# Sliding-window attention into a two-layer block: V loaded in rows of eight tokens and moved to key spans on chip, q and k on 96 partitions, w_out in 8-KB runs

## The chip, the cores and the metric

The kernel runs on one core of a Trainium2 chip. The metric is the device time of one execution in microseconds, the median of several runs. Beside the runs one execution was profiled; the rows in this text come from it. Engines are written as in the profile: PE is the matrix engine and PEld its weight loads, DVE the vector engine, ACT the scalar engine, POOL the GpSimd engine, SP the queue that issues DMAs.

## The reference

Attention over 8 batches of 8 heads, 576 tokens and 64 channels, in which a token sees itself and the 63 tokens before it. Its output, 4608 tokens of 512 channels, goes through two matrices with `h - tanh(h)` between them.

```python
scores = (1 / sqrt(64)) * q @ k.transpose(0, 1, 3, 2)        # 8 x 8 x 576 x 576
mask   = (rel >= 0) & (rel < 64)                             # rel = query - key
attn   = softmax(where(mask, scores, -1e9))
x      = (attn @ v).transpose(0, 2, 1, 3).reshape(4608, 512)
h      = x @ w_in                                            # 512 x 2048
out    = (h - tanh(h)) @ w_out                               # 2048 x 512
```

All inputs and the output are float32; the kernel multiplies in bf16.

## The kernel before

The attention is done for 32 groups `g`, each two heads of one batch (`b, pr = divmod(g, 4)`). q and k of a group come by SP's DMAs (`load_qk`, line 72), 72 partitions of eight tokens, are cast to bf16 (line 82, on POOL but for the first), transposed by eight PE transposes each (`tr`, line 154) and copied out of PSUM to `qT` (lines 158 and 159, the one on ACT, the other on DVE) and `kT` (line 161, ACT). Queries are taken in nine blocks of 64, each against its own 64 keys and the 64 before them, so a block sees 128 keys: nine matmuls `sp` (line 168), three at a time, an Exp on ACT (line 170), one multiplication by the 0-or-1 mask on DVE (`masking`, line 174), and nine matmuls `ov` against V (line 181), three at a time, each followed by a reciprocal of the row sums and two multiplications on DVE (lines 184 and 187). V lies in `vw` with 128 keys on the partitions: the upper 64 partitions hold a block's own keys, loaded straight from HBM with a cast to bf16 by POOL's DMAs (`load_v`, line 91), one run of 64 channels for each key; the lower 64 hold the block before, copied from the upper ones by SP's DMA (`shift_v`, line 97). After each second group `x_tr` transposes the result into `xT` (lines 193 and 201).

The second half works on nine chunks `c` of 512 tokens. For each of 16 tiles `m` of the hidden layer `hp_mm` does four matmuls of 512 columns (`hp`, line 211), ACT takes the tanh (line 214) and DVE the difference `gT` (line 220). `yp_mm` does the second product, four matmuls a step and 16 matmuls to an output tile (line 228); `y_out` copies it on ACT (line 233) and stores it in two DMAs of SP (line 236). w_in and w_out come in four pieces each by POOL's DMAs with a cast (lines 103 and 107).

The order of all of this is written out by hand: time is counted in half steps `h`, two to a step `n = 16 c + m`. An even one does `hp` of step `n`, an odd one `yp` of step `n - 24` (LAG), and `at(h, ...)` adds the attention work in between. Batch 0's attention stands at negative `h`, ahead of the first `hp`; batch 1's is spread over 4 half steps a group, the later ones' over 8. Each engine runs its instructions strictly in the order in which they are written, and so do POOL's and SP's DMA issues. PSUM is shared out in pools: two buffers for `hp`, one for `yp`, two for transposes, two for `sp`, one for `ov`.

## Time and profile before

| | us |
|---|---|
| median of 3 runs | 398.25 |
| lowest and highest run | 393.59, 398.42 |
| the profiled execution's own time | 396.17 |
| its span, first to last instruction | 392.9 |
| PE busy in the span | 329.2 |
| DVE, ACT, POOL busy | 244.2, 184.8, 99.7 |

The profiled execution's time is 3.3 us more than its span; what lies around the span is the same program's start and end. The rows of the trace are in a section below. A row of a timeline begins with its start in us from the span's start and its length, then engine, line, operation, tiles, shapes and count, and in brackets how long the engine sat idle before it and what ended that. In a group of instructions the two numbers behind the bar are the busy time in us and the mean length of one in ns.

### The profile page before, as it was taken

To read this page: it belongs to the slowest core of one execution; us is meant where nothing else is said; L and a number is where in the kernel's file an instruction comes from. 1 tells how busy PE (TensorE), PEld (TensorE's weight loads), DVE (VectorE), ACT (ScalarE), POOL (GpSimd) and SP (SyncE) were. 2 spreads that over 40 slices of the span, in tenths; PEclk is the share of its full clock that TensorE was granted. 3 is DMA by queue.
4 is the path that set the end of the run, shared out by engine and by line. 5 is a ranking of instruction groups with operands and counts; after the bars stand their busy time and mean duration, and the time that the engine had idled before them with its cause. 6 is when DMAs were issued, how large, how long until landed. Compare 5 with 4: busy or idle time off the path is not lost.

```text
span 392.9 us, 6368 instructions
## 1 busy us (share of the span) xinstructions
PE 329.2 (84%) x2384; PEld 179.7 (46%) x2384; DVE 244.2 (62%) x553; ACT 184.8 (47%) x342; POOL 99.7 (25%) x107
## 2 busy tenths in 40 slices
...
GB/s 156 143 187 215 157 135 181 167 97 166 125 123 3 118 151 155 103 117 158 129 119 135 148 106 117 171 133 29 32 41 37 28 53 28 35 47 27 65 69 53
DMA packets 59006, 41.85 MB, mean 107 GB/s; under 512 B 39009, under 2 KB 43105, under 8 KB 58977
## 3 DMA queue, kind: packets, MB, share of 16 engines
q0 software_dynamic: 41536, 8.92, 61.0%
...
## 4 chain that ended last, share of the span: by engine, by line
PE 72%; DMA 13%; DVE 4%; issue 3%; POOL 3%; ACT 3%; SPq 0%; POOLq 0%; ACTq 0%
PE yp L228 32%; PE hp L211 29%; DMA vw<-vw 6%; DMA w_in_sb<-in_moe_w_in_dram 5%; PE ov L181 4%; PE sp L168 3%; PE tp L154 3%; DMA kf<-in_k_dram 2%; DVE xs L187 1%; PE tpx L193 1%; POOL kb L82 1%; DVE gT L220 1%; ACT ysb L233 1%; POOL vw L91 1%; ACT th L214 1%
## 5 line engine op out<-in xcount | busy, mean ns | idle before, releaser
L211 PE MATMUL hp<-xT,w_in_sb 128*128 128x512 bf16 x576 | 152.9, 389 | 3.0 <-DVE gT L220 2.2
L228 PE MATMUL yp<-w_out_sb,gT 128*128 128x512 bf16 x576 | 145.0, 379 | 4.3 <-ACT ysb L233 4.3
L214 ACT ACTIVATE th<-hp 128x512 f32<-128x512 f32 x144 | 86.0, 597 | 131.9 <-PE hp L211 111.4
L220 DVE TENSOR_TENSOR gT<-hp,th 128x512 bf16<-128x512 f32 x144 | 99.5, 692 | 58.8 <-ACT th L214 56.7
L211 PEld LDWEIGHTS <-w_in_sb 128*128 128x128 bf16 x576 | 53.2, 100 | 52.6 <-issue 8.9
L228 PEld LDWEIGHTS <-gT 128*128 128x128 bf16 x576 | 52.4, 98 | 54.0 <-issue 5.9
L181 PE MATMUL ov<-vw,pt 128*128 128x129 bf16 x288 | 36.5, 240 | 41.7 <-DMA vw<-vw 12.9
L187 DVE TENSOR_TENSOR xs<-ov,rc 64x192 bf16<-64x192 f32 x192 | 68.1, 355 | 4.6
L170 ACT ACTIVATE pt<-sp 128x384 bf16<-128x384 f32 x96 | 43.3, 489 | 32.1 <-PE sp L168 31.9
L181 PEld LDWEIGHTS <-pt 128*128 128x128 bf16 x288 | 23.9, 104 | 65.5 <-issue 26.2
L82 POOL CAST qb<-qf 72x1024 bf16<-72x1024 f32 x31 | 34.7, 1121 | 74.2 <-DMA qf<-in_q_dram 49.5
L91 POOL DMA_DIRECT2D vw<-in_v_dram x28 | 25.7, 924 | 68.4 <-PE ov L181 55.0
L82 POOL CAST kb<-kf 72x1024 bf16<-72x1024 f32 x31 | 34.0, 1096 | 20.9 <-DMA kf<-in_k_dram 20.1
L184 DVE RECIPROCAL rc<-ov 128x3 f32<-128x3 f32 x96 | 17.1, 178 | 34.0 <-PE ov L181 31.3
L233 ACT ACTIVATE ysb<-yp 128x512 f32<-128x512 f32 x36 | 21.5, 597 | 28.2 <-PE yp L228 28.2
L168 PE MATMUL sp<-qt,kt 128*128 128x128 bf16 x288 | 30.2, 239 | 1.3 <-ACT kt L161 1.1
L174 DVE TENSOR_TENSOR pt<-pt,mask 128x1152 bf16<-128x1152 bf16 x32 | 30.3, 946 | 0.9
L168 PEld LDWEIGHTS <-kt 128*128 128x128 bf16 x288 | 23.1, 108 | 10.1 <-ACT kt L161 1.8
L161 ACT ACTIVATE kt<-tp 128x576 bf16<-128x576 bf16 x32 | 20.7, 648 | 7.3 <-PE tp L154 7.3
L159 DVE COPY qt<-tp 64x576 bf16<-64x576 bf16 x32 | 14.7, 460 | 13.1 <-ACT qt L158 12.8
L158 ACT ACTIVATE qt<-tp 64x576 bf16<-64x576 bf16 x32 | 20.2, 634 | 0.8 <-PE tp L154 0.8
L154 PE MATMUL tp<-ident,qb 72*128 72x72 bf16 x256 | 14.9, 208 | 5.7 <-POOL mask L127 5.7
...
## 6 DMA issues: line engine op xcount, KB each, us to landing
...
```

The source lines that it names most:

```text
L82: eng.tensor_copy(o, i)
L91: nc.gpsimd.dma_start(out=vw[b % NV][64:128, p0:p1, :, 64 * i:64 * i + 64].rearrange("p r j d -> p (r j) d"), in_=v[b, NP * i + p0:NP * i ...
L154: nc.tensor.transpose(tp[:, e, :], src[:, e, :], ident[:P, :P])
L168: nc.tensor.matmul(sp[:, i, :], kT[g % NR][:, 64 * j:64 * j + 128], qT[g % NR][:, j].rearrange("c h t -> c (h t)"), start=True, stop=True)
L170: nc.scalar.activation(PT[g % NR][:, 3 * grp:3 * grp + 3, :], sp, ACT.Exp, scale=scale)
L174: nc.vector.tensor_tensor(p, p, mask.unsqueeze(1).to_broadcast([128, 2 * NJ, 64]), ALU.mult)
L181: nc.tensor.matmul(ov[:, i, :], PT[g % NR][:, j, :], vw[b % NV][:, pr, j, :], start=True, stop=True)
L187: nc.vector.tensor_tensor(xs[b % 2][r, 3 * grp:3 * grp + 3, pr, :], ov[r, :, r], rc[r].to_broadcast([64, 3, 64]), ALU.mult)
L211: nc.tensor.matmul(hp, w_in_sb[:, ki, m * 128:(m + 1) * 128], chunk_tile(c)[:, ki, :], start=(ki == 0), stop=(ki == 3))
L214: nc.scalar.activation(th, hp, ACT.Tanh)
L220: nc.vector.tensor_tensor(gT[c][:, m, :], hp, th, ALU.subtract)
L228: nc.tensor.matmul(yps[c, s], gT[c][:, m, s * 128:(s + 1) * 128], w_out_sb[:, m, :], start=(m == 0), stop=(m == M - 1))
```

## The change

q and k are taken six tokens to a partition, on 96 partitions, so that a transpose pair is six and six instead of eight and eight. V of two heads is loaded as float32 by POOL's DMAs, eight tokens to a partition on 72 partitions (`load_v`), cast into a bf16 tile `vb` that has a one behind each head's 64 channels (`cast_v`, on DVE for batch 0 and on POOL later), and brought to the key blocks by nine DMAs from SBUF to SBUF on SP (`keys_v`, 64 rows of 520 bf16 values each). The copy to the lower 64 partitions (`shift_v`) covers all eight heads in one DMA, for batch 0 in two DVE copies. w_out is loaded in runs of four whole rows, 8 KB; the hidden units are permuted to fit, so `hp`'s weights are every fourth column of w_in. w_in comes in three pieces. The nine `ov` matmuls of a group go to three PSUM banks and are followed by one reciprocal and two multiplications (`norm`). All of PSUM is one tile whose eight banks are named by number: 0 and 1 for `hp`, 2 for `yp`, 3 for transposes, 4 for scores, 5 to 7 for `ov`. An output tile is stored in one DMA. LAG goes from 24 to 16, and batch 0's attention with all early loads is written as one list of short codes (`play`), of which two lines are shown.

```diff
-    E, P = 8, S // 8
+    E, P = 6, S // 6
+    EV, PV = 8, S // 8
...
-    qk_pool = ctx.enter_context(tc.tile_pool(name="qk", bufs=4))
+    qk_pool = ctx.enter_context(tc.tile_pool(name="qk", bufs=3))
+    v_pool = ctx.enter_context(tc.tile_pool(name="v", bufs=4))
...
-    g_pool = ctx.enter_context(tc.tile_pool(name="g", bufs=3))
-    ps_hp = ctx.enter_context(tc.tile_pool(name="ps_hp", bufs=2, space=PSUM))
-    ps_yp = ctx.enter_context(tc.tile_pool(name="ps_yp", bufs=1, space=PSUM))
-    ps_tp = ctx.enter_context(tc.tile_pool(name="ps_tp", bufs=2, space=PSUM))
-    ps_s = ctx.enter_context(tc.tile_pool(name="ps_s", bufs=2, space=PSUM))
-    ps_ov = ctx.enter_context(tc.tile_pool(name="ps_ov", bufs=1, space=PSUM))
+    g_pool = ctx.enter_context(tc.tile_pool(name="g", bufs=2))
+    psum = ctx.enter_context(tc.tile_pool(name="psum", bufs=1, space=PSUM))
+    ps = psum.tile([128, 8, 512], F32, name="ps")
...
-    w_in_sb = const.tile([128, 4, d_ff], BF16, name="w_in_sb")
+    WIDE = 512, 512, 1024
+    w_in_sb = [const.tile([128, 4, n], BF16, name=f"wi{i}") for i, n in enumerate(WIDE)]
...
-    NV, NR = 2, 3
+    NR, NPT = 2, 4
...
+    vw = [const.tile([128, NJ, H, D + 1], BF16, name=f"vw{i}") for i in range(2)]
+    vb = const.tile([PV, EV, H, D + 1], BF16, name="vb")
+    PT = [const.tile([128, NJ, 128], BF16, name=f"pt{i}") for i in range(NPT)]
...
+    def move(eng, o, i):
+        if eng is nc.scalar:
+            nc.scalar.activation(o, i, ACT.Copy)
+        else:
+            eng.tensor_copy(o, i)
...
-    def load_v(b, p0=0, p1=NP):
-        for i in range(2):
-            nc.gpsimd.dma_start(
-                out=vw[b % NV][64:128, p0:p1, :, 64 * i:64 * i + 64].rearrange("p r j d -> p (r j) d"),
-                in_=v[b, NP * i + p0:NP * i + p1].rearrange("h (j p) d -> p (h j) d", p=64))
-    def shift_v(b, p0=0, p1=NP):
-        w = vw[b % NV].rearrange("p r j c -> p r (j c)")
-        nc.sync.dma_start(out=w[0:64, p0:p1, 129:], in_=w[64:128, p0:p1, :(NJ - 1) * 129])
-    w_in_r = moe_w_in.rearrange("(ko ki) f -> ki ko f", ki=128)
-    w_out_r = moe_w_out.rearrange("(ko ki) f -> ki ko f", ki=128)
-    def load_w_in(i):
-        nc.gpsimd.dma_start(out=w_in_sb[:, :, 512 * i:512 * i + 512],
-                            in_=w_in_r[:, :, 512 * i:512 * i + 512])
-    def load_w_out(i):
-        nc.gpsimd.dma_start(out=w_out_sb[:, 4 * i:4 * i + 4, :], in_=w_out_r[:, 4 * i:4 * i + 4, :])
+    def load_v(b, pr):
+        t = v_pool.tile([PV, 2, EV * D], BF16, tag="vf", name="vf")
+        nc.gpsimd.dma_start(out=t, in_=v[b, pr::NP].rearrange("h (p e) d -> p h (e d)", e=EV))
+        stage[b, pr, "v"] = t
+    def cast_v(b, pr, eng=nc.gpsimd):
+        move(eng, vb[:, :, 2 * pr:2 * pr + 2, 0:D].rearrange("p e h d -> p h e d"),
+             stage.pop((b, pr, "v")).rearrange("p h (e d) -> p h e d", d=D))
+    def keys_v(b):
+        for j in range(NJ):
+            nc.sync.dma_start(out=vw[b % 2][64:128, j].rearrange("p h c -> p (h c)"),
+                              in_=vb[8 * j:8 * j + 8].rearrange("p e h c -> p e (h c)"))
+    def shift_v(b, eng=None):
+        lo, hi = vw[b % 2][0:64, 1:NJ], vw[b % 2][64:128, 0:NJ - 1]
+        if eng is None:
+            nc.sync.dma_start(out=lo.rearrange("p j h c -> p (j h c)"), in_=hi.rearrange("p j h c -> p (j h c)"))
+        else:
+            eng.tensor_copy(lo[:, 0:4], hi[:, 0:4])
+            eng.tensor_copy(lo[:, 4:8], hi[:, 4:8])
+    w_in_r = moe_w_in.rearrange("(ko ki) f -> ki ko f", ki=128)
+    w_out_r = moe_w_out.rearrange("(i p r) d -> i p r d", p=128, r=4)
+    def load_w_in(i):
+        nc.gpsimd.dma_start(out=w_in_sb[i], in_=w_in_r[:, :, 512 * i:512 * i + WIDE[i]])
+    def w_in_tile(ki, m):
+        i = min(m // 4, 2)
+        f = 512 * (m // 4 - i) + m % 4
+        return w_in_sb[i][:, ki, f:f + 4 * 127 + 1:4]
+    def load_w_out(i):
+        nc.gpsimd.dma_start(out=w_out_sb[:, 4 * i:4 * i + 4, :], in_=w_out_r[i])
...
-    def tr(g, which):
+    def tr(g, which, bank, eng=nc.vector):
         src = rows.pop((g, which)).rearrange("p e h d -> p e (h d)")
-        tp = ps_tp.tile([128, E, P], BF16, tag="tp", name="tp")
+        tp = ps[:, bank, :].bitcast(BF16)[:, 0:E * P].rearrange("c (e p) -> c e p", e=E)
         for e in range(E):
             nc.tensor.transpose(tp[:, e, :], src[:, e, :], ident[:P, :P])
         if which == "q":
-            t = tp.rearrange("c e (j a) -> c j e a", a=8)
-            o = qT[g % NR].rearrange("c j h (e a) -> c j h e a", e=E)
-            nc.scalar.activation(o[0:64, :, 0], t[0:64], ACT.Copy)
-            nc.vector.tensor_copy(o[64:128, :, 1], t[64:128])
+            o = qT[g % NR].rearrange("c h (p e) -> c h p e", e=E)
+            t = tp.rearrange("c e p -> c p e")
+            nc.scalar.activation(o[0:64, 0], t[0:64], ACT.Copy)
+            move(eng, o[64:128, 1], t[64:128])
...
-    def scores(g, grp):
-        sp = ps_s.tile([128, 3, 128], F32, tag="s", name="sp")
+    def scores(g, grp, bank):
+        sp = ps[:, bank, 0:384].rearrange("p (i q) -> p i q", i=3)
         for i in range(3):
             j = 3 * grp + i
             nc.tensor.matmul(sp[:, i, :], kT[g % NR][:, 64 * j:64 * j + 128],
-                             qT[g % NR][:, j].rearrange("c h t -> c (h t)"), start=True, stop=True)
-        nc.scalar.activation(PT[g % NR][:, 3 * grp:3 * grp + 3, :], sp, ACT.Exp, scale=scale)
+                             qT[g % NR][:, :, 64 * j:64 * j + 64], start=True, stop=True)
+        nc.scalar.activation(PT[g % NPT][:, 3 * grp:3 * grp + 3, :], sp, ACT.Exp, scale=scale)
...
         b, pr = divmod(g, NP)
-        ov = ps_ov.tile([128, 3, 129], F32, tag="ov", name="ov")
         for i in range(3):
             j = 3 * grp + i
-            nc.tensor.matmul(ov[:, i, :], PT[g % NR][:, j, :], vw[b % NV][:, pr, j, :],
-                             start=True, stop=True)
-        rc = sm_pool.tile([128, 3, 1], F32, tag="rc", name="rc")
-        nc.vector.reciprocal(rc, ov[:, :, 128:129])
+            nc.tensor.matmul(ps[:, 5 + grp, 130 * i:130 * i + 130], PT[g % NPT][:, j, :],
+                             vw[b % 2][:, j, 2 * pr:2 * pr + 2, :], start=True, stop=True)
+    def norm(g):
+        b, pr = divmod(g, NP)
+        ov = ps[:, 5:8, 0:390].rearrange("p n (i h c) -> p n i h c", h=2, c=D + 1)
+        rc = sm_pool.tile([128, 3, 3, 1], F32, tag="rc", name="rc")
+        nc.vector.reciprocal(rc, ov[:, :, :, 0, D:D + 1])
+        xo = xs[b % 2].rearrange("p (n i) r d -> p n i r d", i=3)
         for h in range(2):
             r = slice(64 * h, 64 * h + 64)
-            nc.vector.tensor_tensor(xs[b % 2][r, 3 * grp:3 * grp + 3, pr, :], ov[r, :, r],
-                                    rc[r].to_broadcast([64, 3, 64]), ALU.mult)
-    def x_tr(b, half, w0, w1):
-        tp = ps_tp.tile([128, 5, 128], BF16, tag="tp", name="tpx")
+            nc.vector.tensor_tensor(xo[r, :, :, pr, :], ov[r, :, :, h, 0:D],
+                                    rc[r].to_broadcast([64, 3, 3, 64]), ALU.mult)
+    def x_tr(b, half, w0, w1, bank, eng=nc.vector):
+        tp = ps[:, bank, :].bitcast(BF16)[:, 0:640].rearrange("p (w t) -> p w t", t=128)
...
-            nc.vector.tensor_copy(o[:, half, :, lo - c * WPC:to - c * WPC],
-                                  tp[:, i0:i0 + to - lo].rearrange("p w (h t) -> p h w t", h=2))
+            move(eng, o[:, half, :, lo - c * WPC:to - c * WPC],
+                 tp[:, i0:i0 + to - lo].rearrange("p w (h t) -> p h w t", h=2))
...
-        hp = ps_hp.tile([128, TOK], F32, tag="hp", name="hp")
+        hp = ps[:, m % 2, :]
         for ki in range(4):
-            nc.tensor.matmul(hp, w_in_sb[:, ki, m * 128:(m + 1) * 128], chunk_tile(c)[:, ki, :],
+            nc.tensor.matmul(hp, w_in_tile(ki, m), chunk_tile(c)[:, ki, :],
...
         s, part = divmod(st, 4)
-        if part == 0:
-            yps[c, s] = ps_yp.tile([128, d_model], F32, tag="yp", name="yp")
+        yp = ps[:, 2, :]
         for i in range(4):
             m = 4 * part + i
-            nc.tensor.matmul(yps[c, s], gT[c][:, m, s * 128:(s + 1) * 128], w_out_sb[:, m, :],
+            nc.tensor.matmul(yp, gT[c][:, m, s * 128:(s + 1) * 128], w_out_sb[:, m, :],
                              start=(m == 0), stop=(m == M - 1))
     def y_out(c, s):
         ysb = sm_pool.tile([128, d_model], F32, tag="ysb", name="ysb")
-        nc.scalar.activation(ysb, yps[c, s], ACT.Copy)
-        for u in range(2):
-            r0 = c * TOK + s * 128 + 64 * u
-            nc.sync.dma_start(out=out[r0:r0 + 64, :].rearrange("(a e) d -> e a d", e=E),
-                              in_=ysb[64 * u:64 * u + 64, :])
+        nc.scalar.activation(ysb, ps[:, 2, :], ACT.Copy)
+        r0 = c * TOK + s * 128
+        nc.sync.dma_start(out=out[r0:r0 + 128, :], in_=ysb)
...
-    WIDE = dict(q=0, k=1, s0=4, s1=4, s2=6, mask=8, v0=10, v1=13, v2=15, x0=19, x1=22)
-    TIGHT = dict(q=0, k=1, s0=3, s1=3, s2=4, mask=5, v0=6, v1=7, v2=8, x0=10, x1=11)
...
+    at(-40, play, """
+        q0 v00 v01 v02 v03 i0 q1 c0ap d00d d01d d02d d03d q2 k0 T0 c1pp m0 S0 q3 M0 T1
+        s0d S1 w0 c2pp M1 V0 T2 q4 S2 V1 v10 v11 c3pp M2 T3 v12 v13 V2 S3 X0 M3 V3 X1
...
+        a = 4 * pr
+        at(a, tr, g, "q", 3, nc.scalar)
+        at(a + 1, tr, g, "k", 2)
+        for i in range(3):
+            at(a + 3 + i, scores, g, i, 4)
...
-    LAG = 16 + 8
+    LAG = 16
```

How the order changes at three places. First POOL's instructions from the start, in which `vw` and `vf` are V's tiles, `w_in_sb`, `wi` and `w_out_sb` the weights', and a CAST is one of q or k. Before:

```order
L91 DMA vw_94<-in_v_dram 64x9x64 x4
L125 MEMSET mask 128x64
L127 AFFINE_SELECT mask<-mask 128x64
L129 AFFINE_SELECT mask<-mask 128x64
L82 CAST qb<-qf 72x2x8x64
L82 CAST kb<-kf 72x2x8x64
L91 DMA vw_94<-in_v_dram 64x9x64 x2
L82 CAST qb<-qf 72x2x8x64
L82 CAST kb<-kf 72x2x8x64
L91 DMA vw_94<-in_v_dram 64x9x64 x2
L103 DMA w_in_sb<-in_moe_w_in_dram 128x4x512
```

And POOL's of the changed kernel, from the second piece of V's casts of batch 1 to the second piece of w_out:

```order
L78 COPY vb<-vf 72x2x8x64 x2
L126 DMA wi_85<-in_moe_w_in_dram 128x4x512
L78 CAST qb<-qf 96x2x6x64
L78 CAST kb<-kf 96x2x6x64
L126 DMA wi_86<-in_moe_w_in_dram 128x4x1024
L78 CAST qb<-qf 96x2x6x64
L78 CAST kb<-kf 96x2x6x64
L78 CAST qb<-qf 96x2x6x64
L78 CAST kb<-kf 96x2x6x64
L100 DMA vf<-in_v_dram 72x2x512 x2
L78 CAST qb<-qf 96x2x6x64
L78 CAST kb<-kf 96x2x6x64
```

V's casts now stand on POOL between the casts of q and k, and ahead of w_in's second and third piece.

Second DVE's from batch 0's first V casts (`vb`) on, in the changed kernel; `pt` is the Exp's result, `xs` the attention's output:

```order
L78 COPY vb<-vf 72x2x8x64 x4
L78 COPY qt_97<-ps 64x576
L147 MEMSET qt_98 128x576
L148 MEMSET kt_96 128x32
L150 MEMSET vw_88 64x520
L150 MEMSET vw_89 64x520
L190 TENSOR_TENSOR pt_91<-pt_91,mask 128x1152
L78 COPY qt_98<-ps 64x576
L118 COPY vw_88<-vw_88 64x2080
L119 COPY vw_88<-vw_88 64x2080
L190 TENSOR_TENSOR pt_92<-pt_92,mask 128x1152
L203 RECIPROCAL rc<-ps 128x9
```

Before, the first masking on DVE was followed by three rounds of a reciprocal and two multiplications, and V's casts and the copy to the lower partitions were in DMAs:

```order
L174 TENSOR_TENSOR pt_96<-pt_96,mask 128x1152
L184 RECIPROCAL rc<-ov 128x3
L187 TENSOR_TENSOR xs_105<-ov,rc 64x3x64 x2
L159 COPY qt_104<-tp 64x9x64
L184 RECIPROCAL rc<-ov 128x3
L187 TENSOR_TENSOR xs_105<-ov,rc 64x3x64 x2
```

DVE now does one round a group, and four casts and two copies of V for batch 0.

Third ACT's in batch 1's attention of the changed kernel, one group beside two steps of `hp` (`th` is the tanh; L174 and L76 are the two halves of `qT`, L177 is `kT`, L186 the Exp):

```order
L234 ACTIVATE th<-ps 128x512
L186 ACTIVATE pt_92<-ps 128x384
L234 ACTIVATE th<-ps 128x512
L186 ACTIVATE pt_92<-ps 128x384
L174 ACTIVATE qt_97<-ps 64x576
L76 ACTIVATE qt_97<-ps 64x576
L186 ACTIVATE pt_92<-ps 128x384
L177 ACTIVATE kt_95<-ps 128x576
```

Both halves of `qT` are ACT's there; before, one was DVE's (line 159).

## Rows read from the trace of the kernel before

**Rows 1.** Busy time of each engine in four stretches, granted clock, DMA.
```profile
core 0: us, PE busy (x) PEld busy (x) DVE busy (x) ACT busy (x) POOL busy (x), PEclk, DMA share, GB/s
0.00:51.00 51.00, 16.16 (x154) 12.66 (x155) 22.19 (x59) 12.68 (x22) 28.15 (x42) 1.00 1.73 168
51.00:118.50 67.50, 48.04 (x402) 27.69 (x401) 45.89 (x112) 32.62 (x65) 25.31 (x24) 0.85 1.76 142
118.50:362.50 244.00, 243.32 (x1740) 130.08 (x1737) 176.12 (x383) 135.93 (x250) 46.24 (x42) 1.00 0.71 89
362.50:392.90 30.40, 21.68 (x96) 9.26 (x95) 0.00 (x0) 3.58 (x6) 0.00 (x0) 0.97 0.19 60
```
**Rows 2.** The chain that ended last: start us, length us, what.
```profile
18.92 18.31 DMA w_in_sb<-in_moe_w_in_dram
...
50.30 16.33 DMA vw<-vw
...
86.61 8.60 DMA vw<-vw
...
118.62 0.87 PE yp L228 x4
```
**Rows 3.** POOL's DMA queue on the page: packets, MB, share of 16 engines' span.
```profile
q0 software_dynamic: 41536, 8.92, 61.0%
```
**Rows 4.** The same columns as rows 1, five microseconds of the loading.
```profile
25.00:30.00 5.00, 2.72 (x30) 2.46 (x29) 2.05 (x7) 2.57 (x5) 0.73 (x1) 1.00 1.18 259
```
**Rows 5.** Timeline: first landing, an issue of SP, a cast, V's arrival, the end.
```profile
2.54 0.40 SPq L72 DMA_DIRECT2D qf<-in_q_dram  x1
...
4.54 1.06 ACT L80 ACTIVATE qb<-qf 72x1024 bf16<-72x1024 f32 x1 [2.46 <-DMA qf<-in_q_dram]
...
6.16 0.69 DVE L82 CAST kb<-kf 72x1024 bf16<-72x1024 f32 x1 [1.50 <-DMA kf<-in_k_dram]
...
26.55 0.38 PE L181 MATMUL ov<-vw,pt 128*128 128x129 bf16 x2 [9.15 <-DMA vw<-vw]
...
51.10 3.16 PE L211 MATMUL hp<-xT,w_in_sb 128*128 128x512 bf16 x8
...
384.14 3.61 PE L228 MATMUL yp<-w_out_sb,gT 128*128 128x512 bf16 x16 [0.73 <-ACT ysb L233]
```
**Rows 6.** Groups of instructions: busy us, mean ns, idle before them and its releasers.
```profile
L220 DVE TENSOR_TENSOR gT<-hp,th 128x512 bf16<-128x512 f32 x144 | 99.5, 692 | 58.8 <-ACT th L214 56.7
L214 ACT ACTIVATE th<-hp 128x512 f32<-128x512 f32 x144 | 86.0, 597 | 131.9 <-PE hp L211 111.4 <-ACT pt L170 19.0 <-issue 1.5
L187 DVE TENSOR_TENSOR xs<-ov,rc 64x192 bf16<-64x192 f32 x192 | 68.1, 355 | 4.6
L211 PEld LDWEIGHTS <-w_in_sb 128*128 128x128 bf16 x576 | 53.2, 100 | 52.6 <-issue 8.9
L170 ACT ACTIVATE pt<-sp 128x384 bf16<-128x384 f32 x96 | 43.3, 489 | 32.1 <-PE sp L168 31.9
L82 POOL CAST qb<-qf 72x1024 bf16<-72x1024 f32 x31 | 34.7, 1121 | 74.2 <-DMA qf<-in_q_dram 49.5 <-issue 15.2 <-PE sp L168 4.2
L174 DVE TENSOR_TENSOR pt<-pt,mask 128x1152 bf16<-128x1152 bf16 x32 | 30.3, 946 | 0.9
L161 ACT ACTIVATE kt<-tp 128x576 bf16<-128x576 bf16 x32 | 20.7, 648 | 7.3 <-PE tp L154 7.3
L201 DVE COPY xT<-tpx 128x512 bf16<-128x512 bf16 (+4 forms) x46 | 15.4, 361 | 3.5 <-PE tpx L193 3.1
L159 DVE COPY qt<-tp 64x576 bf16<-64x576 bf16 x32 | 14.7, 460 | 13.1 <-ACT qt L158 12.8
```
**Rows 7.** Timeline: a cast on POOL beside a masking on DVE.
```profile
43.35 1.05 POOL L82 CAST qb<-qf 72x1024 bf16<-72x1024 f32 x1
43.38 2.61 DVE L174 TENSOR_TENSOR pt<-pt,mask 128x1152 bf16<-128x1152 bf16 x1
```
**Rows 8.** Timeline: weight loads of eight transposes.
```profile
58.19 0.33 PEld L154 LDWEIGHTS <-kb 72*128 72x128 bf16 x8
```

More of the change, by code (lines that the diff above doesn't have):

```diff
@@ L78, in cast @@
         i = stage.pop((g, n)).rearrange("p h (e d) -> p h e d", d=D)
-        if eng is nc.scalar:
-            nc.scalar.activation(o, i, ACT.Copy)
-        else:
-            eng.tensor_copy(o, i)
+        move(eng, o, i)
         rows[g, n] = t
@@ L139 @@
-    for pr in range(NP):
-        shift_v(0, pr, pr + 1)
+    def load_v(b, pr):
[9 more added lines that the diff above has]
+                              in_=vb[8 * j:8 * j + 8].rearrange("p e h c -> p e (h c)"))
```

149 lines of the change are left out of this document (91 added, 58 removed).

## The prediction, made before the change was run

> **What bounds the kernel now.** I read four stages first [rows 1]. From 118.5 to 362.5 us PE is busy for 243.3 of 244 us at the full granted clock; then 30 us in which it does the last second products alone. Nothing in the change makes a matmul shorter, so that part can only be had by starting it earlier. The first 118.5 us are the loose part: PE is busy for 16 of the first 51 us and for 48 of the next 67.5, at a mean clock of 0.85. What it waited for there is in the chain of waits [rows 2]: 18.3 us in a load of w_in, then 16.3 and 8.6 us in V's copy from the upper to the lower partitions. The timeline says the same of batch 0: its first matmuls against V go on at 26.55 us, after 9 us of waiting for that copy [rows 5]; the first `hp` is at 51.1 us, the first `yp` at 118.6 [rows 2, 5]. Behind it stands POOL's DMA queue: 41,536 packets for 8.9 MB, 61% of all 16 engines' span [rows 3], nearly all of them V's runs of 64 channels. So I cost the change as a shift of the first `yp`, and leave what follows nearly as it is.
>
> **V and the first loads, up to V in place.** The change asks first for six q and k loads and four of V, each 96 x 2 x 384 or 72 x 2 x 512 values of four bytes, 288 KB: 2.95 MB. The best five microseconds of the loading wrote 259 GB/s [rows 4], the first 51 us 168 [rows 1]: 11.4 or 17.6 us. Some of those 259 were weights, read at twice the bytes that they write, so the engines read more, and half of 11.4 is the lower end. I take 11.4, as V's packets are now 2 KB, and with the queue's start 12 us. V's last cast on DVE is 0.69 [rows 5], then SP issues nine DMAs at 0.4 each [rows 5], 3.6 us; the first load of all was in by 4.5 us [rows 5], so a small one's landing is under 3.7, and I take 2.5. The copy to the lower partitions is two DVE copies of 2080 columns; a masking of 1152 takes 0.95 [rows 6], so 1.7 each at its pace and 0.85 at twice that; half of it overlaps the last landings: 1 us. Sum 12 + 0.7 + 3.6 + 2.5 + 1 = 20 us, where before stands 26.55.
>
> **From there to the first `hp`.** Before, 24.5 us (26.55 to 51.1), a serial round of masking, three times `ov`, reciprocal and multiplications for each group. Now DVE has three maskings at 0.95, two copies of `qT` at 0.46, two of `xT` at 0.36 [rows 6], and four rounds of `norm`. A multiplication of 576 columns has no row: the one of 192 is 0.355, so at most 1.07; the difference `gT` of 512 columns is 0.69 [rows 6], so hardly less than that; 1.7 for two and the reciprocal. Sum 2.8 + 0.9 + 0.7 + 6.8 = 11.2 us. Beside it ACT needs 0.65 + 0.65 + 3 x 0.49 = 2.8 us a group [rows 6], hidden but for the first and the last: 4 us more.
>
> Here POOL comes in. It has V's loads and a dozen casts of 1.1 us in this stretch, and a cast on POOL beside a masking on DVE made the masking 2.61 us [rows 7], while the mean of all 32 is 0.95 [rows 6]. I add 1 us by that mean. The Trainium skill (SBUF — State Buffer, section "SBUF: two separate sides") has DVE and GpSimd share a pair of ports as an exclusive lock for a whole instruction. By that rule the loser always waits, by the mean it does now and then; the rule as a full price is rival two.
>
> First `hp`: 20 + 11.2 + 4 + 1 = 36 us. If DVE never waited it were 31; at the old 24.5 us it were 44.5. w_in's first piece is asked for early enough: by the order POOL issues it behind three casts and the mask, near 10 us, and at 259 GB/s its half megabyte takes 2 us.
>
> **Steps 0 to 7, beside batch 1's attention.** For each group, two steps, ACT has two tanh, three Exp, two halves of `qT` and `kT`: 2 x 0.60 + 3 x 0.49 + 2 x 0.65 + 0.65 = 4.6 us [rows 6]; PE has 2 x 0.87 [rows 2] and some 1.7 of attention, so it is hidden behind ACT. Four groups 18.4 us. The first `hp` will run slowly: before, eight matmuls took 3.16 us [rows 5], against 1.74 later; 1.4 more. Step 8 at 56 us. Without ACT's wait it were 14 us; at the old pace of this stage (24 steps in 67.5 us) 22.5.
>
> **Steps 8 to 15.** Now DVE is the longest: eight differences at 0.69, two maskings, two `norm` of batch 1, two `qT` copies and six of `xT`: 5.5 + 1.9 + 3.4 + 0.9 + 2.2 = 14 us. First `yp` at 70 us, if w_out is there. By then 7.1 MB of q and k, 3.5 of V, 4.2 of weights as written and 2.9 of keys and copies have to move: 17.7 MB in 70 us is 253 GB/s, just the 259 of rows 4, and w_out's last pieces stand on POOL behind V's casts of batch 2. I add 3 us: 73.
>
> **From the first `yp` to the end.** Before, 392.9 - 118.6 = 274.3 us. LAG 16 in place of 24 leaves eight more `hp` steps behind the first `yp`, 8 x 0.87 = 7 us. Attention: the 244 us held 120 steps of 2 x 0.87, 208.8 us, so 35.2 us for some 5.3 batches, 6.6 each; about a quarter batch more is left over now, 1.7 us. At the end PE stops 0.73 us between two output tiles [rows 5], four times and not six: -1.5. Sum 281.5. I put nothing on 96-partition transposes (six of 96 columns for eight of 72, the same columns) nor on the one store in place of two: PE is full, SP is not. `hp`'s weights are now read at every fourth column: PE loads 128 of them in 0.10 us [rows 6] behind a matmul of 0.22, so up to twice that costs nothing; rival four is the rest. In the full stretch DVE and ACT have slack (176 and 136 of 244 us [rows 1]), and POOL's new casts, four a batch at 1.1 us, have more (46 of 244).
>
> **The sum.** 73 + 281.5 = 354.5 us of span; the profiled execution's time is 3.3 over its span: 358 us, where that execution had 396.2. The median of the runs before is 398.25, 2 us higher than the profiled one; I let that be part of the range.
>
> **Rivals.**
> One: the loads stay the bound up to the first `yp`. For it: the 17.7 MB need a rate that only five microseconds of the old trace had, SP and POOL issue in order, and nine small DMAs with waits now stand ahead of q and k on SP. Against it: most of V's small packets are gone from the queue [rows 3]. At the old 168 GB/s it would be 105 us to the first `yp`, in the middle between 73 and that 88: 88 + 281.5 + 3.3 = 373 us.
> Two: DVE waits a whole cast of POOL each time. Three maskings, two copies and four casts of V before the first `hp`, nine times 1.1 us, 10 in place of my 1: 367 us. For it the 2.61 us [rows 7], against it the mean [rows 6].
> Three: one PSUM bank for all transposes. In the full stretch q's transposes are followed by k's in the same bank after one `yp` and one `hp`, 1.74 us. In that time ACT has a tanh and half of `qT`, then DVE the other half: 0.60 + 0.65 + 0.46 = 1.71 us. If each hand-over is 0.5 us late, k's alone cost 24 x 0.5 = 12 us (370), all three of a group 36 us: 394, no change.
> Four, the other side: weight loads at every fourth column take four times as long. 400 ns against 217 of a matmul, 183 x 576 = 105 us: 463 us. It decides from about 300 ns a load on, 84 ns over a matmul, 48 us in all, which is 2% above 398. For it: no row has such a load. Against it: eight loads of 128 columns took 0.33 us [rows 8], 41 ns each; four times that is 165 and stays hidden.
>
> **How the numbers follow.** My forecast 0.65; rival one 0.15, two 0.08, three 0.08 (half of it within 2%), four 0.04. The likeliest is 358. Downwards: loads at twice the rate (-6) and a first `hp` without waits (-5), the 3 us of loads gone: 344. Upwards: the old 24.5 us and the old pace of steps 0 to 7 (+8, +3) give 369, rival one 373 and a little over. Range 343 to 376; outside lie the slow end of rival one, half of three, and four. Faster by over 2%, about what a measurement of this kernel can tell from no change: 0.9; within 2%: 0.05, rival three in full and rival one at its worst; slower: 0.05, rival four and what I have not thought of.
>
> **What would show it.** In the changed trace: batch 0's first matmuls against V near 20 us, the first `hp` near 36, the first `yp` near 73, and from there some 281 us with PE busy throughout. POOL's queue should have under 10,000 packets in place of 41,536: V's runs were one for each of 8 x 8 x 576 keys, 36,864, and are now an eighth of that, 4,608 of 2 KB. Rival one shows as PE waiting for `vw` or `w_out_sb` between 36 and 90 us; two as maskings and V copies of 2 us; three as PE waiting for DVE or ACT at the transposes after 120 us; four as weight loads of `hp` over 217 ns and a PE step over 0.87 us. I am wrong at the root if the stretch behind the first `yp` is more than 5 us longer than 281, or if the first `yp` is past 90 us.

## The result, and the profile after

The changed kernel takes 379.76 us (median of 4 runs, 379.31 to 381.63) beside 395.92 us for the kernel before (390.52 to 398.42): a ratio of 0.9695, 95% interval 0.9611 to 0.978. (The ratio is not that of the two medians: executions of a kernel come in a faster and a slower state, and ratios compare the faster alone, here those of the kernel before at 390.52 and 393.59.) It is faster by 3%, where 358 us and 10% were forecast; 379.76 lies above the range of 343 to 376. The profiled execution took 379.83 us with a span of 378.1. (The section on the change calls V's staging tile float32. It is bf16: POOL's DMA casts on the way, and `cast_v` only moves.)

The same columns as [rows 1], cut where the first `hp` and the first `yp` stand now, then at 120 us:

```profile
0.00:43.40 43.40, 13.97 (x138) 12.16 (x139) 23.95 (x35) 12.53 (x24) 24.08 (x37) 0.88 0.84 171
43.40:82.70 39.30, 28.51 (x254) 17.52 (x253) 25.71 (x42) 26.75 (x52) 18.49 (x23) 0.95 0.90 196
82.70:120.00 37.30, 29.08 (x211) 16.55 (x208) 21.41 (x33) 16.66 (x32) 13.74 (x16) 0.91 0.63 140
120.00:348.00 228.00, 227.44 (x1558) 127.66 (x1556) 149.87 (x241) 126.11 (x233) 52.51 (x63) 1.00 0.43 106
```

The first `yp` came from 118.5 to 82.7 us, 36 us earlier, and the end by only 15. Behind 120 us PE is as full as before. The lost time lies in the third line: PE is busy for 29.1 of 37.3 us, and its clock is granted at 0.91. Before, nothing of this kind stood behind the first `yp`. The chain of waits, in order of time (start, length, what), answers to [rows 2]:

```profile
82.53 3.97 DMA vw<-vb
87.03 4.42 DMA vw<-vw
91.49 0.38 PE ps L196 x2
...
94.38 1.15 PE ps L231 x4
...
104.61 2.15 DVE pt L190
...
110.95 0.97 PE ps L247 x4
```

It is V again, of batch 2 now: the key transfers land at 86.5, SP issues the shift at 87.03, that lands after 4.4 us, and PE has waited 6.69 us. The masking of 2.15 us at 104.61 is another starved one, beside a copy and a cast of POOL; PE waited 1.52 us for it. `hp` at 94.38 takes 1.15 us for its four matmuls where 0.86 is usual: between 90 and 100 us the granted clock is 0.76, so part of that stretch ran at the lower of TensorE's two levels, 1.2 GHz, after PE had been idle. The row at 110.95 is the ninth `yp` step. From there 267.2 us are left, and before it were 274.4 us from the first `yp`, less eight closing steps of 0.87: 267.4. So the pace behind that point is the old one to 0.2 us, and all that the change gives is given ahead of it.

The timeline at the places of [rows 5] (start, length, engine, line):

```profile
14.19 6.54 SPq L110 DMA_DIRECT2D vw<-vb  x9
...
23.29 0.65 PE L196 MATMUL ps<-vw,pt 128*128 128x130 bf16 x4 [1.98 <-DVE vw L119]
...
43.41 0.63 PE L231 MATMUL ps<-xT,wi 128*128 128x512 bf16 x1
```

V of batch 0 is in place at 23.29 us (20 forecast); the first `hp` stands at 43.41 (36). Between them lies one masking, and POOL beside it, as in [rows 7]:

```profile
34.22 2.06 POOL L78 COPY vb<-vf 72x1024 bf16<-72x1024 bf16 x2 [1.86 <-DMA vf<-in_v_dram]
...
34.78 4.61 DVE L190 TENSOR_TENSOR pt<-pt,mask 128x1152 bf16<-128x1152 bf16 x1
36.23 0.78 POOL L126 DMA_DIRECT2D wi<-in_moe_w_in_dram  x1
...
37.00 0.84 POOL L78 CAST qb<-qf 96x768 bf16<-96x768 f32 x1
37.76 0.83 POOL L78 CAST kb<-kf 96x768 bf16<-96x768 f32 x1
38.53 0.76 POOL L126 DMA_DIRECT2D wi<-in_moe_w_in_dram  x1
...
39.44 0.83 PE L196 MATMUL ps<-vw,pt 128*128 128x130 bf16 x6 [5.59 <-DVE pt L190]
```

That masking has 0.75 us of work (what the shortest ones take). It ends at 39.39, 0.8 us behind the cast that ends at 38.59, and did not get in while POOL only issued a DMA from 36.23 on. Of the groups [rows 6] and the queue [rows 3]:

```profile
q0 software_dynamic: 8816, 8.92, 15.6%
...
L231 PEld LDWEIGHTS <-wi 128*128 128x128 bf16 x576 | 60.9, 114 | 46.7 <-issue 5.0
...
L207 DVE TENSOR_TENSOR xs<-ps,rc 64x576 bf16<-64x576 f32 x64 | 48.3, 755 | 1.5
```

The queue has a fifth of its packets, a strided weight load costs 14 ns more behind a matmul of 217, and the multiplications of a division take 48.3 us in all where they took 68.1.

### The profile page after: what moved, and what is told of

Read it like the earlier page. It is cut to its first block, busy times and chain, and to the rows that moved or that the text cites. A ratio compares the mean times of both kernels' runs of the same rounds, so it can differ in the third digit from the quotient of the medians.

```text
span 378.1 us, 6020 instructions
## 1 busy us (share of the span) xinstructions
PE 322.4 (85%) x2256; PEld 184.3 (49%) x2256; DVE 225.1 (60%) x355; ACT 188.7 (50%) x350; POOL 108.8 (29%) x139
## 4 chain that ended last, share of the span: by engine, by line
PE 71%; DVE 5%; DMA 2%; ACT 2%; issue 1%; ACTq 0%; SPq 0%
PE ps L247 32%; PE ps L231 28%; PE ps L196 3%; PE ps L170 3%; PE ps L184 3%; DVE gT L240 2%; DVE pt L190 2%; PE ps L213 1%; DMA vw<-vw 1%; ACT ysb L252 1%; DMA vw<-vb 1%; DVE xs L207 1%; ACT th L234 0%; DVE qt L78 0%; ACT qt L174 0%
## 5 line engine op out<-in xcount | busy, mean ns | idle before, releaser
L231 PE MATMUL ps<-xT,wi 128*128 128x512 bf16 x576 | 149.5, 382 | 3.3 <-DVE gT L240 3.0
L247 PE MATMUL ps<-w_out_sb,gT 128*128 128x512 bf16 x576 | 146.8, 381 | 3.0 <-ACT ysb L252 3.0
L240 DVE TENSOR_TENSOR gT<-ps,th 128x512 bf16<-128x512 f32 x144 | 99.2, 690 | 70.3 <-ACT th L234 69.0
L234 ACT ACTIVATE th<-ps 128x512 f32<-128x512 f32 x144 | 86.2, 598 | 83.9 <-PE ps L231 77.6
L231 PEld LDWEIGHTS <-wi 128*128 128x128 bf16 x576 | 60.9, 114 | 46.7 <-issue 5.0
L186 ACT ACTIVATE pt<-ps 128x384 bf16<-128x384 f32 x96 | 46.1, 490 | 56.0 <-PE ps L184 55.9
L78 POOL COPY vb<-vf 72x1024 bf16<-72x1024 bf16 x28 | 29.2, 1052 | 96.9 <-DMA vf<-in_v_dram 49.4
L207 DVE TENSOR_TENSOR xs<-ps,rc 64x576 bf16<-64x576 f32 x64 | 48.3, 755 | 1.5
L196 PE MATMUL ps<-vw,pt 128*128 128x130 bf16 x288 | 31.8, 230 | 19.3 <-DVE pt L190 9.6
L184 PE MATMUL ps<-qt,kt 128*128 128x128 bf16 x288 | 31.9, 228 | 15.3 <-DVE qt L78 11.4
L78 DVE COPY qt<-ps 64x576 bf16<-64x576 bf16 x28 | 21.3, 760 | 13.3 <-ACT qt L174 13.2
L174 ACT ACTIVATE qt<-ps 64x576 bf16<-64x576 bf16 x32 | 20.3, 635 | 9.0 <-PE ps L170 9.0
L177 ACT ACTIVATE kt<-ps 128x576 bf16<-128x576 bf16 x32 | 20.7, 646 | 7.5 <-PE ps L170 7.4
L78 DVE COPY xT<-ps 128x512 bf16<-128x512 bf16 (+4 forms) x42 | 14.5, 366 | 16.3 <-PE ps L213 16.0
```

Of the source, the lines that this page charges most:

```text
L78: eng.tensor_copy(o, i)
L184: nc.tensor.matmul(sp[:, i, :], kT[g % NR][:, 64 * j:64 * j + 128], qT[g % NR][:, :, 64 * j:64 * j + 64], start=True, stop=True)
L186: nc.scalar.activation(PT[g % NPT][:, 3 * grp:3 * grp + 3, :], sp, ACT.Exp, scale=scale)
L196: nc.tensor.matmul(ps[:, 5 + grp, 130 * i:130 * i + 130], PT[g % NPT][:, j, :], vw[b % 2][:, j, 2 * pr:2 * pr + 2, :], start=True, stop=True)
L207: nc.vector.tensor_tensor(xo[r, :, :, pr, :], ov[r, :, :, h, 0:D], rc[r].to_broadcast([64, 3, 3, 64]), ALU.mult)
L231: nc.tensor.matmul(hp, w_in_tile(ki, m), chunk_tile(c)[:, ki, :], start=(ki == 0), stop=(ki == 3))
```

## The experiments

Each kernel was timed beside the kernel before on one chip, but not all on the same chip. The median of the kernel before was 394.85 to 398.04 us there, so a difference of some 3 us between rows of different chips need not be the edit's.

| run | edit, to which kernel | us | ratio to before, 95% |
|---|---|---|---|
| e1_v2_first | V of batch 2 ahead of w_out, to the changed | 385.16 | 0.9726 (0.9658 to 0.9793) |
| e2_v1_on_act | two V copies to ACT, to the changed | 375.11 | 0.948 (0.942 to 0.954) |
| e3_both | e1 and e2 | 380.41 | 0.962 (0.9556 to 0.9683) |
| e9_pool_clear | e2 and two casts to ACT | 375.71 | 0.9476 (0.9414 to 0.9538) |
| r_after | the changed once more | 378.95 | 0.9644 (0.9572 to 0.9715) |
| e4_v_direct | V straight into place, to the changed | 372.36 | 365.29 to 375.03 us |
| r_v_direct | e4 once more | 370.28 | 0.9411 (0.9343 to 0.948) |
| e14_direct_c4_on_act | two casts to ACT, to e4 | 369.62 | 0.9423 (0.9351 to 0.9495) |
| e11_direct_pool_clear | four casts to ACT, V of batch 2 earlier, to e4 | 373.49 | 0.9381 (0.9304 to 0.9458) |
| e12_direct_v1_late | V of batch 1 behind w_in, to e4 | 374.07 | 0.9449 (0.9376 to 0.9522) |
| e13_v0_staged_only | batch 0's V staged, e9's order, to e4 | 375.19 | 0.9488 (0.9408 to 0.9568) |
| e7_before_lag16 | LAG 16, to the kernel before | 391.38 | 0.9892 (0.9826 to 0.9957) |
| e8_lag24 | LAG 24, to the changed | 388.39 | 0.9779 (0.9685 to 0.9873) |
| e6_w_out_2kb | w_out in 2-KB rows, to the changed | 378.81 | 0.956 (0.9497 to 0.9623) |
| e5_qk72 | q, k on 72 partitions, to the changed | 391.4 | 0.9906 (0.9865 to 0.9948) |
| e16_direct_qk72 | q, k on 72 partitions, to e4 | 378.24 | 0.9588 (0.9543 to 0.9634) |
| e18_direct_qk64 | q, k on 64 partitions, to e4 | 375.09 | 0.944 (0.9368 to 0.9513) |
| e17_one_bank_pv | one bank for `ov`, to e4 | 400.74 | 1.0111 (1.0059 to 1.0162) |

**Is the wait for batch 2's V a matter of order?** First theory: V of batch 2 is late because w_out's pieces and other work stand ahead of it.

```diff
-    ... w2 c6pp s1 q8 c7pp q9 v20 v21 c8pp o0 c9pp o1 v22 v23 d20p d21p o2 qa d22p d23p o3 qb k2 s2
+    ... w2 c6pp v20 v21 v22 v23 s1 q8 c7pp q9 d20p d21p d22p d23p k2 c8pp o0 c9pp o1 qa s2 o2 o3 qb
```

> The changed kernel with batch 2's V loads, V copies and key DMAs put ahead of w_out's loads in the list. Theory Order (V of batch 2 comes late because it stands behind w_out and the q and k casts on POOL): the 6.7 us in which PE waits for vw near 85 us are gone, PE stays at the full clock there, step 24 comes 8 to 9 us earlier (near 102 us), total near 371 us. Theory Rate (the DMA engines are full up to the first yp): PE waits for w_out_sb instead, total 378 to 380 us.

Both theories fell: 385.16 us, slower than the changed kernel, and PE did not wait for w_out instead. The rows of the matmuls against V in its trace, with what ended PE's idle time (us, times):

```profile
DMA vw<-vw: 9.7, 2
DVE pt L190: 8.2, 4
```

There are two waits for the copy now, 4.45 us at 61.5 (batch 1, whose transfers run beside the new loads) and 5.23 at 127.6 (batch 3); the one near 90 us is gone. Moving the loads moved the wait. The same with the edit below (e3_both) read 380.41 us and waited 4.62 us for V at 121.2.

**What the starved masking costs.** Two copies of V of batch 1 go from POOL to ACT; then (e9) two casts of q, k too, and both w_in issues ahead of the casts:

```diff
-    ... S2 V1 v10 v11 c3pp M2 T3 v12 v13 V2 S3 X0 M3 V3 X1 d10p d11p c4pp d12p d13p q5 q6 k1 w1 c5pp q7 w2 c6pp s1 ...
+    ... S2 V1 v10 v11 c3pp M2 T3 v12 v13 V2 S3 X0 d12a d13a M3 V3 X1 d10p d11p c4pp q5 q6 k1 w1 c5pp q7 w2 c6pp s1 ...   e2
+    ... S2 V1 v10 v11 c3pp M2 T3 c4aa v12 v13 V2 S3 X0 d12a d13a M3 V3 X1 d10p d11p q5 q6 k1 w1 w2 c5pp c6pp q7 s1 ...   e9
```

> The changed kernel with the second half of batch 1's V copies on ACT, ahead of the last masking of batch 0, in place of POOL. Theory Port (a masking on DVE waits for POOL's casts): the 4.6 us masking becomes less than 1.5 us and the first hp comes at 39 to 40 us in place of 43.4. By Port alone the total falls to 376 us; by Order the total stays at 379 to 380 us, since V of batch 2 lands as late as before and PE only waits longer for it. If the masking stays at 4 us or more, POOL is not its cause.

> On top of the kernel that casts two pieces of batch 1's V on ScalarE, the casts of q,k group 4 go to ScalarE too, both w_in issues stand ahead of the casts of groups 5 and 6, so that GpSimd has no back-to-back run of casts beside the masking of group 2. Theory (a masking does not start while GpSimd's casts follow each other without a gap): the masking of group 2 takes 0.75 to 1.2 us and not 4.4; first hp 41 to 42.5 instead of 45.3; the whole time 371 to 374 us. Rival (the masking was long for another reason, such as waiting for its data or for the transfers beside it): the masking keeps more than 2.5 us wherever the casts stand, first hp 44 or later, time 375 to 377.

Neither ending of e2 came whole. It took 375.11 us, 4 to 5 less than the changed kernel, but its first `hp` stood at 45.3, later than the 43.41 there. What it gained lies behind the first `yp`: the wait for batch 2's V is 1.96 us in place of 6.69, and the eight steps from there took 20.5 us in place of 28.2. In e2 the masking of group 3 was short, but that of group 2 took its place (start, length, DVE and POOL):

```profile
31.72 4.42 DVE L190 TENSOR_TENSOR pt<-pt,mask 128x1152 bf16<-128x1152 bf16 x1
...
33.72 0.83 POOL L78 CAST qb<-qf 96x768 bf16<-96x768 f32 x1
34.48 0.83 POOL L78 CAST kb<-kf 96x768 bf16<-96x768 f32 x1
35.25 0.76 POOL L126 DMA_DIRECT2D wi<-in_moe_w_in_dram  x1
```

With POOL kept clear, in e9:

```profile
31.04 1.53 POOL L126 DMA_DIRECT2D wi<-in_moe_w_in_dram  x2
...
31.20 1.17 DVE L190 TENSOR_TENSOR pt<-pt,mask 128x1152 bf16<-128x1152 bf16 x1
...
87.15 0.38 PE L196 MATMUL ps<-vw,pt 128*128 128x130 bf16 x2 [4.30 <-DMA vw<-vw]
```

So a masking took 1.17 us beside two DMA issues of POOL, and 4.42 beside its casts in a row, and the first `hp` stood at 41.5 against 45.3, as forecast. It is not a rule without exceptions: in the changed kernel the masking at 30.50 us took 1.18 beside two copies and two casts in a row, and in the kernel before one at 161.88 us took 1.60 beside two DMA issues alone. But the time stayed: 375.71 beside e2's 375.11, and not the 371 to 374 of the theory. The last row shows why: e9 waits 4.30 us for batch 2's V, where e2 waited 1.96. The unedited kernel says something else. 

> The changed kernel once more, unedited, beside the next two. Theory and rival alike: 379 to 381 us, a wait of PE for batch 2's V of 4.5 to 7 us near 90 us.

```profile
PE ps L196 <- DMA vw<-vw: 7.0, 2, 4.7
```

The median is 378.95 us, no other than the first. In its profiled execution the maskings of groups 2 and 3, beside the same copies as before, took 1.09 and 1.04 us, so the order alone does not decide whether one starves. The first `hp` stood at 40.70 and not 43.41, and PE waited for V 4.68 us at 58 (batch 1) and 2.33 at 90 us. That execution took 376.14 us, the shortest of the six and 3.7 less than the first profiled one. So a gain ahead of the appointment with V (the place in the written order where PE asks for it) was lost at it in e9 and kept here; the wait for V is there in both, 7.0 and 6.69 us in all.

**V without its staging.** V is cast by the DMA straight to its keys, in the small packets of before; the nine transfers and the copies go:

```diff
-        t = v_pool.tile([PV, 2, EV * D], BF16, tag="vf", name="vf")
-        nc.gpsimd.dma_start(out=t, in_=v[b, pr::NP].rearrange("h (p e) d -> p h (e d)", e=EV))
+        for i in range(2):
+            nc.gpsimd.dma_start(out=vw[b % 2][64:128, :, 2 * pr + i, 0:D],
+                                in_=v[b, NP * i + pr].rearrange("(j p) d -> p j d", p=64))
...
-            at(32 * b - 78 + 6 * pr, load_v, b, pr)
+            at(32 * b - 72 + 3 * pr, load_v, b, pr)
```

The last two lines also move the loads of batches 3 and on, so the runs with V straight into place price the staging together with the places of its loads.

> The changed kernel with V cast straight from HBM into its place by key, in packets of 128 B as before the change, without the staged rows, the nine key transfers and the vb copies. Theory (the V part carries what LAG does not): first hp at 47 to 51, waits of PE for vw in the first 120 us, time 387 to 392. Rival (the nine transfers, the copies and the starved maskings give back all that the longer packets gain): time 376 to 382.

> The kernel with V straight into place once more, unedited, with more rounds. Theory (the staged V is late for batch 2, and V in small packets is not): no wait for vw near 90 us or one under 4 us, the median 5 us or more under that of the changed kernel beside it. Rival (the first look was low by chance): the two medians within 3 us.

My theory of e4 had the wrong sign, and its rival's 376 was still too long. V straight into place is 8.7 us faster than the change that was to speed it up (370.28 beside 378.95 on one chip, intervals apart). Columns as above, for r_v_direct and then for the changed kernel, over the same stretches:

```profile
0.00:45.00 45.00, 14.57 (x138) 12.99 (x140) 18.68 (x32) 13.26 (x26) 26.40 (x41) 0.98 1.85 172
45.00:84.00 39.00, 29.08 (x257) 18.17 (x261) 24.76 (x42) 27.69 (x53) 22.01 (x30) 0.97 1.79 177
84.00:120.00 36.00, 34.16 (x263) 20.12 (x266) 25.85 (x45) 20.16 (x38) 14.37 (x18) 1.00 1.01 140
```

```profile
0.00:45.00 45.00, 15.31 (x141) 12.59 (x142) 24.09 (x35) 13.30 (x26) 24.08 (x37) 0.87 0.84 172
45.00:84.00 39.00, 28.46 (x258) 17.81 (x257) 25.79 (x42) 27.12 (x52) 18.49 (x23) 0.97 0.89 194
84.00:120.00 36.00, 27.78 (x200) 15.82 (x199) 21.19 (x33) 15.53 (x30) 13.74 (x16) 0.91 0.62 139
```

The small packets keep the DMA engines twice as busy (1.85 against 0.84) at the same 172 GB/s. Only the start waits for it:

```profile
PE ps L193 <- DVE vw L114: 11.7, 1, 11.7
```

V of batch 0 is in place at 27.3 us instead of 23.29, and the first `hp` stands at 45.0 instead of 43.41. Up to 84 us the two are alike again; then PE is busy for 34.2 of 36 us against 27.8, at the full clock. The first `yp` stands at 82.2 and 82.7, the wait for batch 2's V is 1.45 us against 6.69, and from the first `yp` to the end it is 286.5 us against 295.4.

On this kernel the first `hp` was tried once more, by `c4aa` behind T3 in place of `c4pp`: 

> The kernel with V straight into place, with the two casts of q,k group 4 on ScalarE in place of GpSimd, and nothing else moved. Theory (a first hp that comes earlier is kept where V of batch 2 is not late): the masking of group 2 takes under 1.7 us, first hp 43 to 45 instead of 46.2, time 1 to 3 us under the kernel with V straight into place. Rival (the appointment that counts is a later one): the same time within 1 us, whatever the first hp.

The masking took 1.25 us and the first `hp` came at 43.4, as expected; the time is 0.7 us less, which does not part theory from rival. Three other orders, e11_direct_pool_clear, e12_direct_v1_late and e13_v0_staged_only, read 373.5 to 375.2: none gained. Of these only e12 tells something by itself. It puts V of batch 1 behind w_in as before the change: 

> The kernel with V straight into place, but batch 1's V issued behind w_in's second and third piece, as in the kernel before the change. Theory (it is the place of batch 1's V among the loads, and not the form of its packets, that took away the wait for it of before): PE waits 5 us or more for vw between the first hp and the first yp, which are 44 us or more apart instead of 37.5; time 380 to 388 us. Rival (the loads have room behind the first hp either way): no wait over 2 us, time 370 to 376.

The rival held: no wait between the first `hp` and the first `yp`, which are 37.6 us apart. V's place among the loads is not what took the old wait away; what did, no run here shows. (e12 waits 3.4 us for batch 2's V at 89 us.)

**What carries the gain, then.** LAG, `LAG = 16` in the kernel before and `LAG = 16 + 8` with a third `g` buffer in the changed one:

> The kernel before with LAG 16 in place of 24, nothing else. If the earlier yp is a gain of its own, because steps 16 to 24 leave PE time for eight yp steps of 0.87 us each: 389 us. If those steps have no room, or w_out is late for them: 396 us, no change. If yp in between delays the attention of batch 2: above 396 us.

> The changed kernel with the distance between hp and yp put back from 16 to 24 steps (and the third g buffer that this needs). Theory (from the first yp on each pair of steps costs the same, so steps taken before it without a yp beside them are lost): 4 to 7 us slower, 384 to 387. Rival (a longer lead covers the wait for batch 2's V, 6.7 us, and so pays for itself): 376 to 381.

391.38 us and 388.39: LAG is worth 5.2 us on the one kernel and 8.6 on the other (6.9 without the longest of e8's four runs, 392.24; 7 forecast); the longer lead did not pay for itself. w_out by `"(i r p) d -> i p r d"`, with weights of 128 adjacent columns:

> The changed kernel with w_out read in rows of 2 KB and w_in's columns in order (no permuted rows, weights of 128 adjacent columns). Theory (the runs of w_out and the order of the columns lie beside other work): weight loads of hp go back from 114 to 100 ns, the time stays at 378 to 381 us and the first yp within 1 us of 82.7. Rival (the 8-KB runs bring the first yp forward, or relieve the queue that batch 2's V stands in): first yp or the wait for batch 2's V later by 3 us or more, time 383 to 387.

378.81 us; weight loads of 99 ns; the first `yp` at 84.3, as its first `hp` stood at 45.5. The runs and the permutation are worth nothing here, in either direction. Then the rows of q and k, `E, P = 8, S // 8` in place of 6, with V staged and with V direct, and 9:

> The changed kernel with q and k on 72 partitions (eight tokens a row, eight transposes a tile) instead of 96 (six). Theory (the 96 partitions save two transposes a tile and some of each copy, beside other work behind the first hp and 1 to 2 us ahead of it): 380 to 384 us. Rival (they carry much of the change's gain, through ACT and DVE in the stretch with batch 1's attention): 386 to 392 us.

> V straight into place and q,k on 72 partitions, so that of the change there remain the order of the first loads, the one set of banks, the distance of 16 steps and w_out's runs. Theory (the 96 partitions bring q, k and what stands behind them in earlier, whatever the form of V): 376 to 384 us, first hp or first yp 3 us or more later than the 45.0 and 82.2 of V straight into place with 96 partitions. Rival (they gain 12 us only because the staged V is late and every delay of it is paid): 369 to 373 us.

> V straight into place and q,k on 64 partitions, nine tokens a row. Theory (a load uses as many of the 16 DMA engines as divide its rows: 16 for 96 rows and for 64, 12 for 72): between 5 and 10 us the DMA engines write 220 GB/s or more, as with 96 rows (233) and not as with 72 (170), and the first cast of q on ScalarE starts at 4.1 to 4.3 us and not at 4.5; the whole time is open, since GpSimd's casts are longer on fewer partitions. Rival (the more rows the faster): 170 GB/s or less there, the first cast at 4.5 us or later, time above the 378 us of 72 rows.

With 72 partitions the changed kernel takes 391.4 us, and with V direct 378.24 instead of 370.28: 12 and 8 us, where the prediction put nothing. The rival held in e5, where PE waits 16.3 us for V in place of 6.7, and the theory in e16, with the first `hp` at 47.9 and the first `yp` at 87.1. Between 5 and 10 us of the program, on 96, 72 and 64 partitions (V direct; r_v_direct, e16, e18), the last column is GB/s:

```profile
5.00:10.00 5.00, 1.30 (x12) 0.97 (x12) 0.59 (x1) 1.13 (x3) 4.52 (x8) 1.00 1.30 233
```

```profile
5.00:10.00 5.00, 1.30 (x16) 1.05 (x16) 0.60 (x1) 1.47 (x3) 4.89 (x8) 1.00 1.74 170
```

```profile
5.00:10.00 5.00, 1.29 (x18) 1.07 (x18) 0.60 (x1) 1.77 (x3) 4.93 (x8) 1.00 1.41 212
```

72 rows load at 0.73 of the rate of 96, and 64 at 0.91. That more rows are always faster is thereby ruled out, and 64 rows gave the shorter time too (375.09). The theory came short on its other number: 212 and not 220, and the first cast of q at 4.80 us, later than the 4.51 of 72 rows. The Trainium skill (DMA: Bandwidth & Descriptors, section "Why a DMA increments its semaphore by 16 and not by 1") has a transfer use the largest number of engines up to 16 that divides its rows: 12 for 72, 16 for 96 and 64. The 0.73 agrees with 12/16; the 0.91 and the late first cast it does not explain, and they stay open. Fewer rows also make POOL's casts longer: 1.04 us on 72, 0.83 on 96, 1.16 on 64. How much of the 8 to 12 us is the load rate and how much these casts, no run parts: on 64 rows the first `hp` stood at 41.8 us, ahead of the 45.0 on 96, and yet the time is 4.8 us longer than there.

Last the three banks for `ov`: all three products of a group into bank 5, each divided before the next.

```diff
-            nc.tensor.matmul(ps[:, 5 + grp, 130 * i:130 * i + 130], ...
+            nc.tensor.matmul(ps[:, 5, 130 * i:130 * i + 130], ...
+        nc.vector.reciprocal(rc, ov[:, :, 0, D:D + 1])
+            nc.vector.tensor_tensor(xs[b % 2][r, 3 * grp:3 * grp + 3, pr, :], ov[r, :, h, 0:D], rc[r].to_broadcast([64, 3, 64]), ALU.mult)
```

> V straight into place on 96 partitions, but the three products of a group against V go into one PSUM bank, each divided before the next is written, as in the kernel before (two multiplications of 64 x 192 and a reciprocal three times a group, not two of 64 x 576 and one). Theory (the three banks took away PE's waits for DVE's multiplications, some 1.1 us twice a group, in front of the first yp): PE waits for xs of 1.0 to 1.2 us twice a group again up to the first yp, the first yp 6 us or more later than 82.2, time 376 to 384 us. Rival (ACT or the loads set the pace there anyway): first yp within 3 us, time 369 to 374.

400.74 us: 30 us, far over the theory's 6 to 14. Its timeline has the wait twice a group, and the waits of PE over 120 to 350 us (us in total, times, longest) show what the theory left out:

```profile
67.15 0.33 PE L193 MATMUL ps<-vw,pt 128*128 128x130 bf16 x3 [1.03 <-DVE xs L200]
68.51 0.42 PE L193 MATMUL ps<-vw,pt 128*128 128x130 bf16 x3 [1.03 <-DVE xs L200]
```

```profile
PE ps L193 <- DVE xs L200: 8.7, 32, 0.5
```

The first `hp` is at 53.1 and the first `yp` at 99.8, 8.1 and 17.6 us later; behind it PE now waits in the full stretch as well. DVE also has more to do in e17, 240.3 us in all in place of 213.3, and no run parts that from the bank itself. The kernel before had one bank too, with its products at other places: it lost nothing in its full stretch [rows 1], and waited some 1.1 us for the multiplications ahead of its first `yp`. So 30 us is the price of one bank, with its shorter multiplications, within the new order, and not what three would have given to the kernel before.

## Why the prediction was wrong

Its sum was 73 + 281.5 + 3.3. Measured: 82.7 + 295.4 + 1.7.

- **V in place, 20; it was 23.3.** The step that failed is "nine DMAs at 0.4 each", 3.6 us: SP took 6.54 us, 0.61 to 1.05 each. The 0.4 was the row of a load of 72 rows, and these move 64 pieces of 1040 bytes. The loads were in at 13.2 us where 12 was put, and the last copy of V took 0.97 where 0.69 was put; the landing and the last copy to the lower partitions gave 1 us back.
- **First `hp`, 36; it was 43.4.** Of the 7.4 us, 3.3 come from the step above and 4.1 from the way on. There the three maskings took 6.55 us, one of them 4.61, where 3.85 was put, the 1 us for POOL included. That is rival two, put at its mean. That POOL's work beside it makes a masking long is borne out by e2 and e9, but the price is another than one cast each time: a row of them or, as at 30.50 us, hardly any. The row behind the price had it already. The cast of [rows 7] ends at 44.40, and the masking goes on to 45.99, past a second cast:

```profile
44.33 1.05 POOL L82 CAST kb<-kf 72x1024 bf16<-72x1024 f32 x1
```

The Trainium skill (SBUF — State Buffer, section "SBUF: two separate sides") has the ports locked for a whole instruction. The 2.61 us here span two casts and the 4.42 and 4.61 us six POOL instructions, which that section does not state. How much of these us reaches the end differs: none of the 3.8 us of e9, while the execution of r_after with its first `hp` 2.7 us earlier ended 3.7 us earlier.
- **`hp` to `yp`, 37; it was 39.3.** Right to 2.3 us, in part because two errors cancel: steps 0 to 7 took 18.6 us (20 put), steps 8 to 15 20.6 (17 put, 3 of them for loads). The reasons are those given: ACT is busy for 9.18 of the 10 us from 50 to 60, DVE for 8.32 from 70 to 80. But in r_after it was 45.2 us, with 4.68 of waiting for batch 1's V, for which nothing was put.
- **From the first `yp` to the end, 281.5; it was 295.4.** Here the argument failed, and by its own sign (more than 5 us over 281) at the root. With 267.4 us from the ninth step on, the prediction had 14.1 us for the first eight steps; they took 28.2. "PE is full" was carried over from a stage where V comes long ahead to one where it is not in yet: V of batch 2 passes a load, a copy on POOL (to 76.7 us), nine transfers (issued to 84.0, landed at 86.5) and a shift (in at 91.4), and I priced that path for batch 0 only. PE waits 6.69 us for it and then runs for some us at the lower clock. r_v_direct shows its size: 8.9 of the 13.9 us go with the staging. The other 5 are mostly attention: in those eight steps of r_v_direct PE is busy for 18.23 of 19.96 us at the full clock, 13.9 for the steps themselves and so 4.3 for attention, where 1.7 was put; the other 1.7 it waits. How the loss is shared out varies: in r_after the stretch was 288.5 us, behind a first `yp` at 85.9.
- **96 partitions, nothing.** "The same columns" was true for PE and beside the point: 8 to 12 us (e16, e5), by faster loads and shorter casts, which no run parts. The bound "259 GB/s" came from a stretch in which weights were loaded too; between 5 and 10 us the kernel before wrote 190 GB/s and the changed one 240.
- **LAG, 7:** right (5.2 and 6.9 to 8.6). w_out's runs beside other work: right (e6).
- **Rivals.** Three fell: transposes through one bank leave PE busy for 227.4 of 228 us. Four fell: 114 ns. One, the loads as bound up to the first `yp`, was nearest in time (373), and its sign, PE waiting for `vw` between 36 and 90 us, is there: from 84.8 us, and in r_after at 58. But the rate of the loads is not what PE waits for: r_v_direct moves no more GB/s up to 84 us (172 and 177, beside 172 and 194) and waits 1.45.

So the gain of 16 us (by the medians; 12 by the ratio) is the sum of parts of both signs: LAG and the partitions of q and k bring 5 to 12 us each (the partitions measured on the changed kernels alone), the banks a part that was not measured on the kernel before, w_out nothing, and V's staging, which the change is named after, costs 8.7, though it brings V of batch 0 in 4.0 us earlier. Without it the kernel is the best of those tried: 370.28 us, and 369.62 with two casts on ACT.
